# An RWKV-5 attention and MLP kernel in one program: weights loaded as whole rows, one interleaved pair instead of two, more turns by DMA, a new hand-written order

## The chip, the cores and the metric

One core of one Trainium2 chip runs the whole program. The metric is device time in microseconds (us), the median of several runs. The profile shown is of one execution; its times count from that execution's first instruction.

## The reference

For each of 4 batches and 8 heads (head width 48, 768 positions) a state of 48 x 48 decays by `w` and takes up `k` times `v` at every position; `r` reads it. The result, 384 wide, then goes through a layer norm and a two-layer MLP with a residual.

```python
for t in range(S):
    cur = einsum('bhd,bhe->bhde', u[None] * k[t], v[t])
    y[t] = einsum('bhd,bhde->bhe', r[t], state + cur)
    state = w[None, :, :, None] * state + einsum('bhd,bhe->bhde', k[t], v[t])
x = y as (4, 768, 384)
xn = (x - mean(x)) / sqrt(var(x) + 1e-6) * g_ln
out = x + maximum(xn @ w_ch1, 0) @ w_ch2          # 384 -> 1536 -> 384
```

## The kernel before

The 3072 positions are cut into 24 chunks (tiles) of 128, six to a batch. All inputs are fp32 in memory, the matmuls run in bf16. The program is a list of steps, `PLAN`, written out by hand; each entry is `name,index,engine`, with `s` for ACT, `v` for DVE, `g` for POOL, `-` for PE or a DMA issued by SP. Every engine takes its steps in the order of that list. So the list sets all that is queued behind what.

**Loading.** `LK`, `LR` and `LV` (L352, L355, L358) fetch one chunk of k, r or v, 192 KB in runs of 192 bytes. `LK2`, `LR2`, `LV2` (L371, L374, L377) fetch two chunks at once, 384 KB, and put two neighbouring positions on one partition, so that a run is 384 bytes. Pairs below `PAIRS` are kept in that interleaved order through the whole attention (`AT2`, `Y2`, `AM2`, L435, L497, L523); from there on only r comes in pairs, and `TCr` (L411) puts it back in order while it copies the turned r out of PSUM.

**Attention of a chunk.** `SK`/`SR` (and `SKH`, `SRH`, `SR2` for interleaved pairs) scale k and r. Both are then turned: by PE (`TRk`, `TRr`, L400) with a copy out of PSUM (`TCk`, `TCr`), or by a DMA (`TDk` L422, `TDr` L427). `AT` is the score matmul, `AM` its mask, `S` the state update and the bonus sums (copied by `CC2`), `ZU`/`ZD` the decayed state, `Y` the output, `X` adds the bonus term.

**MLP of a tile.** `XN` centres x and `SQ` sums its squares. x is turned by PE and copied (`LT` L627, `XT` L633) or by a DMA (`LTD` L621). `UP` (L637) is one PSUM bank of the first matmul: 12 matmuls for a group of one tile, 6 wider ones for a group of two. Step number is 16 x group + bank. `RL` (L654) takes the bank out through a relu, on ACT or DVE. There are two such banks. `DN` (L666) is four matmuls of the second layer, and step number is 4 x tile + third. `RS` (L610) makes the reciprocal deviation: on ACT as an `Ln` and an `Exp` (L613, L614), on POOL as a power. `OT` applies it and adds x, `STO` stores.

**Weights.** `LW1` (L334) fetches a third of the first weight, 768 KB; `SW` (L337) scales a ninth of it to bf16: step i is for columns n = i / 3 and input rows kc = i mod 3. `UP` with bank n of a one-tile group needs the three `SW` of that n. `IW2` (L348) fetches a third of the second weight from POOL's queue with a cast.

**Start.** `WF` fetches w, `LN` takes its logarithm on ACT (L284), `WBM` spreads it by a matmul, and `FK2`, `FR2`, `FK`, `FR`, `WL` take `Exp` of multiples of it. `DU` steps are matmuls on zeros that keep PE busy. `TL` (L231) is one instruction on ACT, in the ninth place of the list, ahead of `LN`:

```python
    def TL(i, e):
        nc.scalar.preload_act_table_set("natural_log_exp_and_others")
```

Of the kernel before, what the change touches and what calls it, by code (L numbers as in the profile page):

```python
# [21 lines left out]
TCk,0,s TRr,1,- LV2,1,- CV2,0,s UW,0,v Q2,0,v AT2,0,- DU,1536,- FR,0,s TCr,1,v LK,4,- WL,0,s SR2,2,g AM2,0,v S,0,- AT2,1,-
LK,6,- CC2,0,s DU,512,- ZU,0,v TRk,1,- AM2,1,v DU,512,- VB2,0,g S,1,- TCk,1,s LK,7,- DU,512,- TRr,2,- LW1,1,- SR2,3,v DU,512,-
Y2,1,- TCr,2,s LW1,2,- LV,5,- Q2,1,v Y2,0,- SK,4,g ZU,1,v UGC,0,s LV,4,- CV2,1,s X,1,v TRr,3,- SK,5,g X,0,v DU,512,-
AT2,3,- TCr,3,s DU,512,- AM2,3,v SK,7,g S,2,- XN,1,s AT2,2,- XN,0,g CC2,1,v ZU,2,v SQ,1,s DU,512,- VB2,1,g TRk,2,- AM2,2,v
S,3,- LW1,0,- TCk,2,s DU,512,- SK,6,v LT,1,- Y2,2,- SQ,0,s SW,5,g XT,1,v SW,3,s LV,6,- LT,0,- SW,4,v TRk,3,- Q2,2,g
ZU,3,v DU,1024,- SW,6,s LK,8,- XT,0,v Y2,3,- SW,7,s TCk,3,v X,2,v SW,8,s AT,5,- AT,4,- X,3,v XN,2,g DU,512,- UP,2,-
AM,5,v XN,3,s IW2,0,g LV,7,- UP,1,- RL,2,s Q2,3,g AM,4,v LT,2,- CV2,2,s DU,512,- UP,17,- RL,1,s XT,2,v S,4,- RL,17,s
LR2,4,- UP,34,- SW,0,v SW,2,s AT,6,- CC2,2,v ZU,4,v SW,1,s VB2,2,g AT,7,- AM,6,v LK,9,- Y,4,- RL,34,s UP,0,- IW2,1,g
X,4,v UP,18,- RL,0,s AM,7,v IW2,2,g Y,5,- XN,4,s LT,3,- UP,32,- RL,18,s RS,1,g LV,8,- X,5,v LT,4,- UP,33,- RL,32,s  # L30
XT,3,v XN,5,g DU,512,- CV2,3,v LV,9,- UP,16,- RL,33,s XT,4,v SK,8,v S,6,- DN,0,- SR2,4,v CC2,3,s RL,16,s UP,48,- SQ,5,s
ZU,6,v UP,64,- VB2,3,v RL,48,s TRr,4,- SQ,3,s Y,6,- SK,9,g DN,1,- RS,3,s X,6,v RL,64,s UP,66,- RS,0,g TDk,4,- SQ,2,s
DN,2,- RS,2,g LT,5,- S,7,- OT,0,v RL,66,s UP,49,- XN,6,s XT,5,v UP,50,- RL,49,v TCr,4,s LR2,6,- DN,4,- ZU,7,v UP,80,-
ZD,7,v LK,10,- CV2,4,g RL,50,v Y,7,- RL,80,s DN,5,- X,7,v LV,13,- DN,6,- Q2,4,v XN,7,s UP,65,- SQ,4,s OT,1,v LV,11,-
AT,8,- SQ,6,s SR2,6,v AT,9,- DN,8,- RS,6,s LR2,5,- AM,8,v RS,4,s DN,9,- SQ,7,s LK,11,- S,8,- DN,10,- ZU,8,v LV,10,-
UP,82,- CC2,4,s OT,2,v VB2,4,g LK,12,- LT,6,- AM,9,v Y,8,- RL,82,s DN,12,- STO,0,- RL,65,s SK,10,g DN,13,- XT,6,v LK,13,-
X,8,v DN,14,- ZD,8,g LV,12,- S,9,- UP,96,- OT,3,v SK,11,g ZU,9,v UP,98,- RL,96,s SR2,5,v Y,9,- TDk,5,- SQ,8,s DN,16,-
CV2,5,v LT,7,- TRr,5,- SK,12,v DN,17,- X,9,v TCr,5,s RL,98,v LK,15,- UP,97,- XN,9,g LK,14,- XT,7,v ZD,9,g UP,81,- RL,97,s
LR2,7,- XN,8,s SK,13,g UP,112,- RL,81,s LTD,8,- DN,18,- RS,7,s Q2,5,v TRr,6,- OT,4,v UP,114,- SK,15,g TCr,6,s RL,112,v STO,1,-
S,10,- CV2,6,g DN,20,- CC2,5,s TDk,6,- RL,114,s SK,14,v AT,10,- RS,5,s AT,11,- ZU,10,v DN,21,- SR2,7,g AM,10,v UP,113,- STO,3,-  # L40
DN,22,- AM,11,v RL,113,s TDk,7,- Y,10,- VB2,5,g UP,129,- OT,5,v TRr,7,- RL,129,s LR,19,- UP,130,- ZD,10,g X,10,v UP,133,- LV,14,-
Q2,6,v RL,130,s DN,24,- TCr,7,v STO,2,- S,12,- DN,25,- CC2,6,s LV,15,- XN,10,s VB2,6,g ZU,12,v AT,12,- SQ,9,s AT,13,- STO,5,-
AM,12,v Y,11,- RL,133,s DN,26,- Q2,7,g LK,16,- X,11,v UP,128,- OT,6,v XN,11,s Y,12,- UP,131,- X,12,v LK,17,- DN,28,- AM,13,v
SR,19,g CV2,7,s S,13,- DN,29,- LTD,9,- ZU,13,v SQ,12,s DN,30,- ZD,13,g RL,128,s Y,13,- OT,7,v AT,15,- SQ,11,s LR2,8,- AT,14,-
X,13,v UP,132,- STO,4,- SK,17,g RL,131,v SQ,13,s LR,18,- S,14,- AM,15,v LV,17,- XN,13,s DN,32,- LV,16,- XN,12,s DN,33,- ZU,14,v
RL,132,s SK,16,v UP,144,- CC2,7,v AM,14,v LTD,10,- VB2,7,g UP,147,- RL,144,s DN,34,- SQ,10,s SR2,8,v TDk,8,- Y,14,- RS,8,s UP,145,-
RL,147,s OT,8,v TRr,8,- ZD,14,v UP,148,- TCr,8,s RL,145,v RL,148,v DN,36,- LK,18,- X,14,v DN,37,- CV2,8,v XN,14,s S,15,- UP,149,-
ZU,15,v LK,19,- UP,161,- ZD,15,g RL,149,v LV,18,- DN,38,- RL,161,s Q2,8,v STO,7,- Y,15,- LV,20,- UP,146,- SK,18,g X,15,v STO,6,-
AT,16,- RL,146,s AT,17,- XN,15,v LR,20,- UP,164,- RS,9,g OT,9,v LTD,11,- AM,17,v UP,160,- RL,164,s RS,10,g DN,40,- RL,160,v S,16,-
SK,19,v UP,163,- SR,18,v CC2,8,s TDk,9,- UP,165,- ZU,16,v RL,163,s AM,16,v DN,41,- ZD,16,g RL,165,s DN,42,- VB2,8,g LR,21,- UP,162,-  # L50
OT,10,v TDr,9,- Y,16,- RL,162,v DN,44,- X,16,v DN,45,- XN,16,g UP,176,- LV,19,- SR,20,g DN,46,- RL,176,s STO,8,- Y,17,- OT,11,v
UP,178,- LK,20,- X,17,v DN,48,- Q2,9,v LK,21,- UP,177,- XN,17,g SR,21,v DN,49,- LTD,12,- RL,177,s RL,178,v DN,50,- CV2,9,v AT,19,-
OT,12,v AT,18,- SK,20,g STO,9,- UP,180,- AM,18,v STO,11,- S,18,- SK,21,g RL,180,s UP,181,- CC2,9,v ZU,18,v DN,52,- VB2,9,g AM,19,v
RL,181,s STO,10,- UP,179,- SQ,16,s TDk,10,- DN,53,- RL,179,s Y,18,- SQ,17,s TDr,10,- DN,54,- X,18,v UP,194,- OT,13,v UP,195,- STO,12,-
RL,194,s LK,23,- Y,19,- SQ,14,s DN,56,- LR,23,- X,19,v SQ,15,s DN,57,- XN,18,s RS,11,g UP,197,- RL,195,s DN,58,- XN,19,s S,19,-
RL,197,s LTD,13,- UP,196,- OT,14,v SQ,19,s Q2,10,v DN,60,- RL,196,s ZU,19,v LV,21,- UP,193,- LR,22,- ZD,19,g LK,22,- UP,192,- RL,193,s
SK,23,g AT,20,- SQ,18,s STO,13,- AT,21,- AM,20,v LV,22,- DN,61,- RL,192,s SR,23,g LV,23,- RS,12,s DN,62,- CV2,10,g UP,208,- OT,15,v
UP,210,- AM,21,v RL,208,s DN,64,- SR,22,v S,20,- RL,210,v UP,212,- TDr,11,- CC2,10,v DN,65,- SK,22,v VB2,10,g ZU,20,v DN,66,- Y,20,-
TDk,11,- OT,16,v UP,209,- X,20,v DN,68,- RL,209,s ZD,20,v STO,14,- S,21,- XN,20,g RL,212,v CV2,11,s DN,69,- LTD,14,- ZU,21,v SQ,20,s
DN,70,- UP,213,- RS,13,s OT,17,v STO,16,- UP,211,- STO,15,- Y,21,- RL,211,s DN,72,- X,21,v DN,73,- Q2,11,v SQ,21,s AT,23,- ZD,21,v  # L60
RL,213,s AT,22,- XN,21,v S,22,- LTD,15,- UP,224,- ZU,22,v AM,22,v DN,74,- ZD,22,g RL,224,s UP,226,- CC2,11,s RS,14,s OT,18,v VB2,11,g
UP,225,- AM,23,v STO,18,- DN,76,- RL,225,s Y,22,- RL,226,s DN,77,- X,22,v DN,78,- XN,22,g UP,240,- LTD,16,- OT,19,v Y,23,- RL,240,s
DN,80,- X,23,v STO,17,- UP,242,- XN,23,v STO,19,- SQ,23,s LTD,17,- DN,81,- RL,242,s DN,82,- SQ,22,s UP,257,- RS,17,s OT,20,v RS,16,g
UP,241,- RL,257,s RS,15,g DN,84,- RL,241,s UP,258,- DN,85,- RL,258,v UP,256,- DN,86,- RL,256,v UP,272,- OT,21,v UP,273,- STO,21,- DN,88,-
RL,273,v DN,89,- RL,272,v DN,90,- UP,274,- OT,22,v DB,0,- STO,22,- RL,274,s DB,1,- STO,20,- DA,0,- DB,2,- DA,1,- OB,23,v DA,2,-
# [5 lines left out]
def kernel(  # L71
# [122 lines left out]

    psum = {}
# [135 lines left out]
                func=ACT.Exp, scale=float(L),  # L331
            )

    def LW1(n, e):  # L334
        nc.sync.dma_start(out=w1_f[n][:], in_=w1_src[:, n])

    def SW(i, e):  # L337
        n, kc = divmod(i, CK)
        o, s = w1_sb[n][kc][:], w1_f[n][:, kc]
        g = g_neg[:, kc : kc + 1]  # L340
        if e == "s":
            nc.scalar.activation(out=o, in_=s, func=ACT.Copy, scale=g)  # L342
# [440 lines left out]
```

## Time and profile before

| | us |
|---|---|
| median of 3 runs | 149.03 (148.55 to 149.23) |
| span of the profiled execution | 147.5 |
| PE busy | 141.5 |
| DVE busy | 112.3 |
| ACT busy | 82.4 |
| POOL busy | 72.0 |

Busy time of an engine is the time in which one of its instructions ran; PE's contains the matmuls on zeros, and its matmuls overlap, so that the mean duration of one is longer than the step from one to the next. The chain of waits goes back from the last instruction to what released each piece of work; its pieces of PE work give the time that a step takes when PE runs without a pause. "SPq" is SP issuing DMAs.

### The profile page before, as it was taken

To read this page: it belongs to the slowest core of one execution; us is meant where nothing else is said; L and a number is where in the kernel's file an instruction comes from. 1 tells how busy PE (TensorE), PEld (TensorE's weight loads), DVE (VectorE), ACT (ScalarE), POOL (GpSimd) and SP (SyncE) were. 2 spreads that over 40 slices of the span, in tenths; PEclk is the share of its full clock that TensorE was granted. 3 is DMA by queue.
4 is the path that set the end of the run, shared out by engine and by line. 5 is a ranking of instruction groups with operands and counts; after the bars stand their busy time and mean duration, and the time that the engine had idled before them with its cause. 6 is when DMAs were issued, how large, how long until landed. Compare 5 with 4: busy or idle time off the path is not lost.

```text
span 147.5 us, 4689 instructions
## 1 busy us (share of the span) xinstructions
PE 141.5 (96%) x1943; PEld 111.1 (75%) x1943; DVE 112.3 (76%) x206; ACT 82.4 (56%) x181; POOL 72.0 (49%) x96
## 2 busy tenths in 40 slices
...
GB/s 112 300 242 240 192 339 187 283 243 215 220 95 231 202 225 165 264 205 258 164 192 196 195 235 124 173 204 227 197 112 191 182 142 154 82 46 119 8 99 111
DMA packets 85097, 27.18 MB, mean 184 GB/s; under 512 B 80338, under 2 KB 83540, under 8 KB 85076
## 3 DMA queue, kind: packets, MB, share of 16 engines
...
q0 software_dynamic: 432, 1.18, 4.3%
q8 instruction: 15, 0.25, 0.7%
q14 instruction: 6, 0.05, 0.1%
q10 hardware_dynamic: 2, 0.00, 0.0%
HBM read 18.88 MB, written 4.72 MB: 160 GB/s over the span
## 4 chain that ended last, share of the span: by engine, by line
PE 65%; SPq 13%; DMA 11%; DVE 6%; POOL 1%; issue 1%; DVEq 0%
PE o L674 28%; PE hp L646 25%; DMA kf<-in_k_dram 6%; DMA w_f<-in_moe_w_ch_dram 5%; SPq L374 4%; SPq L352 3%; PE at L544 3%; PE y L583 2%; SPq L358 2%; PE y L481 2%; PE y L575 2%; SPq L371 1%; SPq L377 1%; DVE hT L664 1%; PE y L460 1%
## 5 line engine op out<-in xcount | busy, mean ns | idle before, releaser
L646 PE MATMUL hp<-xT,w_sb 128*128 128x128 bf16 (+1 forms) x648 | 57.1, 237 | 0.8 <-ACT w_sb L342 0.7
L662 ACT ACTIVATE hT<-hp 128x512 bf16<-128x512 f32 x55 | 32.4, 594 | 40.5 <-PE hp L646 39.7
L646 PEld LDWEIGHTS <-w_sb 128*128 128x128 bf16 x648 | 49.3, 114 | 5.1 <-ACT w_sb L342 1.3
L674 PE MATMUL o<-w_sb,hT 128*128 128x384 bf16 x276 | 53.0, 326 | 0.0
L674 PEld LDWEIGHTS <-hT 128*128 128x128 bf16 x276 | 25.0, 97 | 12.0
L553 DVE TENSOR_TENSOR A<-at,mask 128x1024 bf16<-128x1024 f32 x20 | 24.2, 1216 | 2.1 <-PE at L544 2.1
L492 POOL TENSOR_TENSOR Vb<-vf,cc 128x768 f32<-128x768 f32 x11 | 16.5, 1498 | 14.9 <-ACT cc L200 8.5
L730 DVE SCALAR_TENSOR_TENSOR ot<-o,rs,x 128x384 f32<-128x384 f32 x23 | 14.1, 615 | 12.3 <-PE o L674 7.0
L205 POOL TENSOR_TENSOR sk<-kf,Fk 128x384 bf16<-128x384 f32 x13 | 13.6, 1053 | 8.5 <-DMA kf<-in_k_dram 7.9
L597 ACT ACTIVATE sqj<-x,sm 128x384 bf16<-128x384 f32 x24 | 14.6, 609 | 2.2 <-DVE x L590 2.2
L205 POOL TENSOR_TENSOR Z<-ZS,WLZ 128x384 bf16<-128x384 f32 x8 | 8.0, 1002 | 15.4 <-DVE ZS L565 15.4
L590 DVE SCALAR_TENSOR_TENSOR x<-y,Vb 128x384 f32<-128x384 f32 x20 | 11.0, 552 | 4.5 <-PE y L583 4.1
L664 DVE TENSOR_SCALAR hT<-hp 128x512 bf16<-128x512 f32 x17 | 11.5, 684 | 3.4 <-PE hp L646 3.3
L279 PE MATMUL o<-warm 128*128 128x512 bf16 x33 | 11.3, 427 | 1.0 <-DVE warm L228 1.0
L200 ACT COPY trr<-at 128x512 bf16<-128x512 bf16 (+1 forms) x13 | 9.1, 764 | 4.4 <-PE at L400 4.4
L205 DVE TENSOR_TENSOR sr<-rf,Fr 128x768 bf16<-128x768 f32 (+1 forms) x11 | 9.5, 870 | 1.6 <-DMA rf<-in_r_dram 1.6
L205 POOL TENSOR_TENSOR sr<-rf,Fr 128x384 bf16<-128x384 f32 (+1 forms) x5 | 6.6, 1325 | 7.0 <-DMA rf<-in_r_dram 7.0
L604 ACT ACTIVATE xn<-x,sm 128x384 bf16<-128x384 f32 x13 | 7.8, 609 | 2.3 <-DVE x L590 2.3
L606 POOL TENSOR_SCALAR xn<-x,sm 128x384 bf16<-128x384 f32 x8 | 5.3, 665 | 7.6 <-DVE x L590 7.5
L205 DVE TENSOR_TENSOR q<-trk,trr 128x1024 bf16<-128x1024 bf16 x9 | 7.5, 837 | 1.4 <-ACT xn L604 1.0
L481 PE MATMUL y<-vv,sk 128*128 128x96 bf16 (+1 forms) x96 | 7.3, 204 | 0.3 <-ACT vv L200 0.2
L205 DVE TENSOR_TENSOR sk<-kf,Fk 128x384 bf16<-128x384 f32 (+1 forms) x10 | 7.4, 747 | 0.0
...
## 6 DMA issues: line engine op xcount, KB each, us to landing
...
```

The lines of the kernel that those rows point to most:

```text
L205: engines[e].tensor_tensor(out=out, in0=in0, in1=in1, op=ALU.mult)
L279: nc.tensor.matmul(out=warm_ps[0][:].rearrange("p (a t) -> p a t", a=4), lhsT=warm[:], rhs=rhs, start=True, stop=True)
L481: nc.tensor.matmul(out=t[:, q * E2 : (q + 1) * E2].rearrange("p (e d) -> p e d", e=2), lhsT=lhs, rhs=rhs, start=first, stop=True, skip_gro ...
L492: engines[e].tensor_tensor(out=Vb2(g).rearrange("p (x h d) -> p x h d", x=2, h=H), in0=vals, in1=cc2(g)[:].unsqueeze(3).to_broadcast([P, 2 ...
L553: nc.vector.tensor_tensor(out=AA(i)[:].rearrange("p e q t -> p (e q) t"), in0=psum["at", i][:].rearrange("p e q t -> p (e q) t"), in1=mask ...
L590: nc.vector.scalar_tensor_tensor(out=xx(i)[:], in0=psum["y", i][:, :C], scalar=1.0, in1=Vb(i), op0=ALU.mult, op1=ALU.add, accum_out=sm[i][:],)
L597: nc.scalar.activation(out=sqj[:], in_=xx(i)[:], func=ACT.Square, bias=sm[i][:], scale=-float(C), accum_out=sq[g][:, j : j + 1])
L646: nc.tensor.matmul(out=t[:, a * gw : (a + 1) * gw], lhsT=w1_sb[n][kc][:, fb::FB], rhs=xT(g)[:, :size, kc, :], start=(kc == 0), stop=(kc == ...
L662: nc.scalar.activation(out=o, in_=s, func=ACT.Relu)
L664: nc.vector.tensor_relu(out=o, in_=s)
L674: nc.tensor.matmul(out=psum["o", i][:, :C], lhsT=hT(g)[:, fk, j * P : (j + 1) * P], rhs=w2_sb[d][:, a, :], start=(fk == 0), stop=(fk == FK ...
L730: nc.vector.scalar_tensor_tensor(out=ot(i)[:], in0=psum["o", i][:, :C], scalar=rs[g][:, j : j + 1], in1=xx(i)[:], op0=ALU.mult, op1=ALU.add,)
```

## The change

- `PAIRS` is 1 instead of 2: only chunks 0 and 1 are kept interleaved. Chunks 2 and 3 come as single loads of k and v, with `AT`, `Y`, `AM`; their r still comes as a pair and is put in order by `TCr`.
- The first weight is fetched as whole rows: `LW1,kc` takes 128 rows of 1536 numbers (768 KB) instead of a third of the columns of all rows. The bytes are the same, but any `SW` of a column third now needs the row block that it is in, so the first `UP` needs all three loads.
- The list is new. The three `LW1` stand behind the first pair's loads, k of chunks 2 and 3 and (two of them) v of chunks 2 and 3. `IW2,1` and `IW2,2` stand near the start of POOL's steps.
- r of chunks 12 to 17 comes as single loads and is turned by `TDr` 6, 7, 8; `TRr` and `TCr` 6, 7, 8 go. Tiles 6 and 7 are turned by `LTD`; `LT` and `XT` 6, 7 go.
- `XT` 0 to 4 move from DVE to ACT; `SW` runs 7 times on ACT and twice on POOL (before: 6 on ACT, 2 on DVE, 1 on POOL).
- `TL` stands in the middle of the list, behind `RL,149`, instead of ahead of `LN`. Between `LN` and `TL` the list has `RS` on ACT for groups 1, 0, 3, 4, 2, 5 and 9.

```diff
-PAIRS = 2
+PAIRS = 1
...
+ML,0,v WF,0,s LN,0,s MI2,0,g MW,0,v MO,0,v DU,3072,- WBM,0,- FK2,0,s MM,0,g MP,0,g MP,1,g FR2,0,s MZ,0,v MP,2,g MM2,0,g MP,4,g
+LK2,0,- MP,3,g FK2,1,s LR2,0,- UF,0,- LV2,0,- LR2,1,- LK,3,- LG,0,- LK,2,- LW1,1,- LV,2,- LV,3,- LW1,0,- LW1,2,- LR2,2,- LK,4,-
+LK,5,- LV,4,- LK,7,- LV,5,- UWR,0,v DU,4096,- COL,0,- FR2,1,s SKH,1,v MI,0,g FR,0,s FK,0,s SRH,0,v CV2,0,v SRH,1,v UW,0,s
+UGC,0,s WL,0,s SKH,0,g IW2,1,g SR2,1,g IW2,2,g MP,5,g SK,2,g SK,3,g TRk,0,- TCk,0,v DU,512,- TRr,0,- TCr,0,v DU,1536,- AT2,0,-
+Q2,0,v DU,512,- S,0,- AT2,1,- CC2,0,s AM2,0,v ZU,0,v VB2,0,g IW2,0,g CV2,1,g S,1,- TRr,1,- AM2,1,v Y2,0,- ZU,1,v X,0,v TRk,1,-
+SW,7,s SW,4,s TCr,1,s TCk,1,v Q2,1,v SW,0,g SW,1,g Y2,1,- SR2,2,g AT,3,- X,1,v XN,0,s LT,0,- XT,0,s S,2,- AT,2,- SQ,1,s XN,1,s
+CC2,1,s ZU,2,v DU,1536,- S,3,- AM,2,v SW,3,s RS,1,s SQ,0,s ZU,3,v LT,1,- Y,2,- XT,1,s SW,2,s SW,5,s UP,1,- VB2,1,v AM,3,v X,2,v
+RL,1,s UP,16,- UP,0,- RL,16,s DN,4,- TRr,2,- Y,3,- XN,2,g SK,4,g RL,0,v X,3,v SK,5,v XN,3,g CV2,2,g SW,6,s SW,8,s LT,2,- UP,17,-
...
+AM,5,v UP,32,- SK,7,v RL,32,v SK,6,g Y,4,- LT,3,- SQ,2,s XT,3,s TRr,3,- UP,2,- VB2,2,g X,4,v RL,2,s TRk,3,- Y,5,- UP,49,- DN,2,-
+TCr,3,v XN,4,s SQ,3,s TCk,3,s LT,4,- UP,48,- XT,4,s RS,0,s X,5,v RL,49,v Q2,3,v OT,0,v CV2,3,g SK,9,g SR2,4,g SK,8,g UP,33,-
+AT,6,- AT,7,- RL,48,s S,6,- RL,33,s CC2,3,s RS,3,s SQ,4,s RS,4,s DN,8,- DN,9,- XN,5,g VB2,3,g AM,6,v ZU,6,v AM,7,v Y,6,- TRr,4,-
+UP,64,- DN,10,- X,6,v RL,64,s TCr,4,s TDk,4,- LT,5,- Y,7,- UP,50,- LV,9,- LV,8,- LK,11,- XT,5,v UP,80,- XN,6,v X,7,v XN,7,v
+RL,50,s RS,2,s OT,2,v AT,8,- AT,9,- S,7,- ZU,7,v Q2,4,v AM,9,v SK,10,g SK,12,g RL,80,s SR2,5,g ZD,7,g CV2,4,s SK,11,v AM,8,v
+UP,66,- UP,65,- DN,12,- RL,66,s S,8,- SQ,6,s RL,65,s UP,81,- RL,81,s CC2,4,s LV,12,- LTD,6,- STO,0,- LK,13,- LTD,7,- TDk,5,-
...
+ZU,10,v SR,13,g RL,112,s UP,113,- LTD,8,- STO,1,- UP,128,- CC2,5,s SQ,8,s RS,5,s RL,113,s SQ,7,s RL,128,s DN,26,- TDk,6,-
+TDr,6,- LK,15,- LR,14,- LV,13,- LK,14,- SR,15,v VB2,5,g ZD,10,g UP,131,- Y,10,- UP,114,- RL,114,s RL,131,s OT,6,v X,10,v DN,20,-
...
+Y,13,- OT,7,v X,13,v XN,13,g TDk,7,- TDr,7,- UP,145,- UP,146,- S,13,- LK,17,- LK,16,- STO,6,- LTD,10,- STO,7,- LR,17,- RL,145,s
+SQ,12,s SQ,13,s RL,146,s RS,9,s DN,40,- UP,147,- AT,14,- AT,15,- UP,149,- Q2,7,g ZU,13,v CV2,7,v S,14,- RL,147,s RL,149,s TL,0,s
...
-    w1_f = [const.tile([P, CK, FW], FP32, name=f"w1_f{n}") for n in range(NW)]
+    w1_f = [const.tile([P, F], FP32, name=f"w1_f{kc}") for kc in range(CK)]
...
-    w1_src = moe_w_ch1.rearrange("(kc p) (n f) -> p n kc f", p=P, n=NW)
+    w1_src = moe_w_ch1.rearrange("(kc p) f -> p kc f", p=P)
...
-    def LW1(n, e):
-        nc.sync.dma_start(out=w1_f[n][:], in_=w1_src[:, n])
+    def LW1(kc, e):
+        nc.sync.dma_start(out=w1_f[kc][:], in_=w1_src[:, kc])
...
-        o, s = w1_sb[n][kc][:], w1_f[n][:, kc]
+        o, s = w1_sb[n][kc][:], w1_f[kc][:, n * FW : (n + 1) * FW]
```

78 lines of the change are left out of this document (30 added, 48 removed).

## The prediction

> **What bounds the kernel now.** I read the chain of waits first, then the chain in order of time, then the windows.
>
> ```profile
> span 147.5 us, 4689 instructions
> PE 65%; SPq 13%; DMA 11%; DVE 6%; POOL 1%; issue 1%; DVEq 0%
> ```
>
> PE is two thirds of the chain. The rest of the chain (SP's issues and DMA) is the start.
>
> ```profile
> 26.10 0.25 PE L646 MATMUL hp<-xT,w_sb 128*128 128x128 bf16 x1
> 28.97 0.83 PE L646 MATMUL hp<-xT,w_sb 128*128 128x128 bf16 x12
> 46.87 0.55 PE at L544 x16
> 48.83 0.18 PE y L460 x8
> 49.01 0.19 PE y L481 x4
> 49.20 0.65 PE o L674 x4
> 49.85 0.67 PE hp L646 x12
> 50.52 0.17 PE at L631 x3
> 50.69 0.17 PE y L575 x4
> 50.86 0.20 PE y L583 x8
> 59.64 0.45 PE at L400 x8
> 70.55 0.65 PE hp L646 x6
> 143.08 0.33 PE o L689 x4
> 144.44 0.42 DVE ot L705
> ```
>
> The first two rows (timeline) are the first `UP` matmul, at 26.10, and the end of the third `UP`, `UP,17`, at 29.80. The others (chain) are what each step costs when PE runs without a pause: `UP` 0.67 (one tile) or 0.65 (two), `DN` 0.65, two `AT` 0.55, `S` 0.18 for its bonus sums and 0.19 for its state, `LT` 0.17, `Y` 0.17 + 0.20, a `TR` 0.45, a half `DN` 0.33. I counted what the old list has behind `UP,17`: 33 x 0.67 + 36 x 0.65 `UP`, 69 `DN`, 18 `AT`, 20 `Y`, 16 `S`, 5 `TR`, 5 `LT`, 6 halves: 112.4 us. PE took from 29.8 to 144.4, so 114.6. From about 30 us on PE has gaps of only 2.2 us in all, and 3.1 us follow its last step. **The bound is PE's remaining work, counted from when `UP` starts in earnest.**
>
> **The new list on the same scale.** Behind its first `UP` (`UP,1`) stand 36 x 0.67 + 36 x 0.65 `UP`, 69 `DN`, 20 `AT`, 21 `Y`, 16 `S`, 6 `TR`, 4 `LT`, 6 halves: 115.6 us. The three `TRr` (1.35) and two `LT` (0.34) that go are already left out of it. With the same gaps and the same end the span is T + 115.6 + 2.2 + 3.1 = **T + 120.9**, where T is the time of `UP,1`; it ties with 147.5 at T = 26.6.
>
> **When the weights are there.** `UP,1` needs `SW` 3, 4 and 5, so all three row blocks.
>
> ```profile
> 0.00:5.00 5.00, 4.03 (x11) 1.73 (x12) 1.75 (x9) 2.00 (x3) 4.09 (x22) 1.00 0.62 161
> 5.00:10.00 5.00, 4.55 (x66) 2.87 (x64) 3.81 (x8) 4.22 (x7) 0.64 (x5) 1.00 1.03 257
> 10.00:15.00 5.00, 4.71 (x81) 3.02 (x79) 4.43 (x7) 3.03 (x6) 2.85 (x2) 1.00 1.01 252
> 15.00:20.00 5.00, 5.00 (x138) 3.69 (x136) 4.71 (x10) 4.22 (x8) 2.98 (x4) 1.00 0.97 220
> 20.00:25.00 5.00, 4.74 (x115) 3.46 (x113) 4.82 (x8) 2.63 (x6) 3.96 (x5) 1.00 0.98 296
> 25.00:30.00 5.00, 4.23 (x78) 3.36 (x73) 4.35 (x9) 4.34 (x8) 4.96 (x4) 1.00 0.92 240
> 30.00:35.00 5.00, 5.00 (x107) 4.80 (x106) 4.55 (x11) 4.10 (x8) 3.51 (x6) 1.00 1.13 235
> 35.00:40.00 5.00, 5.00 (x85) 4.41 (x83) 3.96 (x8) 3.98 (x12) 0.78 (x1) 1.00 1.13 217
> L335 SPq DMA_DIRECT2D w_f<-in_moe_w_ch_dram x3: 486/769/5583, 15.9 to 19.6; - x3
> DMA to landing us min/median/max: 7.4/8.6/9.8
> ```
>
> The last column of the windows is GB/s. From 5 to 30 us the mean is 253, and 0.8 MB have moved before. The old list has 6.29 MB ahead of and in its last `LW1`: 5 + 5.49 / 253 = 26.7; it landed at 19.6 + 9.8 = 29.4, 2.7 late. The new list has, up to `LW1,2`, four pair loads (1.57 MB), four single loads (0.79), the weight (2.36) and, on POOL's queue beside it, the second weight (1.18): 5.90 MB, so 5 + 5.09 / 253 = 25.1. But the second weight is read as fp32 and counted as bf16: in the two windows in which it moved, 30 to 40 us, the rate was 235 and 217, which is 1.1 us lost: **26.2**. Bounds: 28.9 with the lateness of the old one; 20.5 if the second weight's bytes all come behind. I take 26.2, since fewer loads queue behind it. The row block before it lands some 2 us sooner, as the first two loads did (15.9 + 7.4 and, by the median of 8.6, about 25.3): 24.2. That the first weight moves in runs of 6 KB instead of 2 KB I count as nothing to 1.5 us of gain: the 20-25 us window, the one with most weight bytes, has 296 GB/s against 253.
>
> ACT then has, in list order, `SW,3`, `RS,1`, `SQ,0`, `XT,1`, `SW,2`, `SW,5`, and `UP,1` waits behind the last.
>
> ```profile
> L662 ACT ACTIVATE hT<-hp 128x512 bf16<-128x512 f32 x55 | 32.4, 594 | 40.5 <-PE hp L646 39.7
> L597 ACT ACTIVATE sqj<-x,sm 128x384 bf16<-128x384 f32 x24 | 14.6, 609 | 2.2 <-DVE x L590 2.2
> L597 ACT ACTIVATION_READ_ACCUMULATOR sqj<-x,sm 128x1 f32 x24 | 4.6, 190 | 0.0
> L604 ACT ACTIVATE xn<-x,sm 128x384 bf16<-128x384 f32 x13 | 7.8, 609 | 2.3 <-DVE x L590 2.3
> L342 ACT ACTIVATE w_sb<-w_f,g_neg 128x512 bf16<-128x512 f32 x6 | 4.0, 713 | 2.2 <-DMA w_f<-in_moe_w_ch_dram 2.2
> L613 ACT ACTIVATE rs<-sq,epsc 128x1 f32<-128x1 f32 x7 | 2.1, 295 | 0.1
> L614 ACT ACTIVATE rs<-rs 128x1 f32<-128x1 f32 x7 | 1.4, 203 | 0.2
> 17.89 1.34 ACT L200 COPY trr<-at 128x512 bf16<-128x512 bf16 x2 [0.47 <-PE at L400]
> L200 ACT COPY cc<-y 128x16 f32<-128x16 f32 x7 | 1.2, 173 | 3.4 <-PE y L481 2.9 <-DVE ZS L565 0.5
> ```
>
> `SW` is 0.71, `SQ` 0.80 (609 + 190 ns), `RS` 0.50 (295 + 203), `RL` 0.59, a `TCr` two copies with 1.34 from start to end, `CC2` 0.17. `XT` on ACT is in no row; between 0.59 and 0.71 (the rows around it) I take 0.6, the row of that size (L604). So 24.2 + 0.71 + 0.50 + 0.80 + 0.6 = 26.8, then two `SW`: T = 28.2, and T + 120.9 = **149.1, with nothing else changed**: the earlier weights are used up by the wait for all three and by PE having done less before them.
>
> **The table load.** This is where I see the change decided.
>
> ```profile
> 1.26 1.28 ACT L231 ACT_TABLE_LOAD   x1 [1.26 <-PEq L767]
> 2.55 0.52 ACT L284 ACTIVATE ln_all<-w_row 1x384 f32<-1x384 f32 x1
> ```
>
> The old run has one table load, x1, 1.28 us, ahead of ACT's first `Ln`; the `RS` on ACT (seven in the two rows above, three more for groups of two) then run `Ln` and `Exp` with nothing between (idle before the seven 0.1 and 0.2 us in all). The new list has this instruction behind `RL,149`. `LN`, the `Exp` steps and seven `RS` stand before it. No row shows what stands in front of an `Ln` when the named set is not loaded. Lower bound: one load serves all, nothing added. Upper bound: a load made for an `Ln` brings no `Exp` and the other way round; then each change from one to the other is a load: `LN`, `FK2`, 7 x 2, and `TL`, 17 loads. I take the upper bound, because the program asks for its set by a name with both functions in it, while a load made on need knows only the function that needs it. Per load I take 1.28; with the idle time in its own row, 1.26, the most is 2.54.
>
> The first two cost nothing: `LN` has its load where `TL` was, and the `Exp` load lies beside `WBM`. Each of the seven `RS` grows from 0.50 to 0.50 + 2 x 1.28 = 3.07, and what queues behind it on ACT are `RL`s; PE has two banks, so it stops at the third `UP` or at a `DN` that needs the relu. Place by place, PE's work until it must wait against ACT's until it lets it go:
>
> - `RS,1`: ahead of `UP,1`, PE has nothing else: **2.6**. T = 30.8.
> - `RS,0`: PE from the end of `UP,48`: `UP,33`, two `AT`, `S,6`, `DN,8` = 2.2, then `DN,9` needs `RL,33`. ACT: `XT,4`, `RS`, two `RL` = 4.9, begun 0.7 sooner: 4.2. Loss **2.0**.
> - `RS,3`, `RS,4`: PE has `DN,9`, `Y,6`, `TRr,4`, `UP,64`, `DN,10`, `LT,5`, `Y,7`, `UP,50` = 3.8, then no bank. ACT: `CC2`, `RS`, `SQ`, `RS`, `RL,64` = 7.7. Loss **3.9**.
> - `RS,2`: `UP,66` starts at 2.1, then `UP,65` needs `RL,80`, at 1.34 + 0.59 + 3.07 + 0.59 = 5.6; without the loads 3.0. Loss **2.6**.
> - `RS,5`: `UP,131` needs `RL,113`; PE has 0.65 of other work, ACT is late by 1.4 without the loads already. Loss **2.6**.
> - `RS,9`: PE has 3.1 until `DN,41` needs `RL,147`, ACT 5.8, without the loads 3.2. Loss **2.6**.
> - `TL` itself: two `DN`, `S,15`, two `UP` hide 1.28. Nothing.
>
> Sum 16.3. From below: behind `UP,1` up to `TL` the list has 53.6 us of PE and 44.6 of ACT (with `TL`); six `RS` make ACT 60.0, so if every wait were shared the loss is 2.6 + 6.4 = 9.0. From above, with 2.54 a load, 33. I take 16.3, since the row of L662 shows 39.7 us of waits for PE: ACT follows PE bank by bank, with no stock to live on.
>
> The Trainium skill, page "ScalarE: Activation LUTs", section "What ACT_TABLE_LOAD costs", gives 1283 ns for the load, as the row here, and about 1380 ns of drain with it for a switch. The row shows `LN` 0.01 us behind the load, so no drain behind it; one ahead of it no run here shows. By 2.66 us a switch the estimate would be 14 x 1.38, some 19 us more.
>
> **The rest, costed at nothing.**
>
> ```profile
> trr<-sr SPq DMA_TRANSPOSE x3, 4.9
> xT<-xn SPq DMA_TRANSPOSE x10, 3.0
> ```
>
> `TDr` 6 to 8 and `LTD` 6, 7 take 4.9 and 3.0 us to land, and stand 5 to 6 us of PE's work ahead of their use; `LTD,6` waits for `XN,6` with a store, `LK,13`, `LTD,7`, `TDk,5` and r of pair 6 behind it on SP. Five pair loads become ten single loads, twice the runs for the same bytes, while SP also has five more turns. A slower PE gives these more room; without that cover up to 2 us at each of the five turns. Three `TCr` less free ACT of 4.0 us where it waits for PE anyway.
>
> **The sum.** 30.8 + 120.9 + (2.0 + 3.9 + 2.6 + 2.6 + 2.6 = 13.7) = 165.4 us of span. The median of the runs is 149.03 for 147.5 of span, 1.5 more: **166.9**.
>
> **The rivals.**
>
> - **One load serves all.** Against it: the named set. For it: nothing in the trace speaks of loads on need. T = 28.2, span 149.1, **150.6 us**; 145 to 154 by the bounds of the landing. The Trainium skill, page "ScalarE activation tables: per-element evaluation and per-set limits", section "Table sets in the compiler and the runtime", says that loads are placed block by block, by the greedy longest run; by that rule this is the case. No row of the old run can show it. Chance 0.07.
> - **Faster: one load serves, and the weights come early.** The place is ACT's `SW,2` and `SW,5`. At the 296 GB/s of the 20-25 window the last block lands at 22.2, T = 24.2, span 145.1, **146.6 us**. It decides where T is below 26.6. Against it: the second weight shares the engines. Chance 0.04.
> - **A load costs twice**, by the 2.54 above: 14 more loads x 1.26 = 17.6 on ACT and, as ACT has no stock, on PE: **184 us**. Against it: the idle time in that row ends with PE's sequencer, not with the load. Chance 0.07.
>
> **How the numbers follow.** Forecast 0.82, rivals 0.07, 0.04, 0.07. The forecast's own range is 153 to 178 (T between 25 and 33.5, losses behind it between 6.4 and 22). To leave out no more than 2 in 10 the range goes up to 180. A measurement of this kernel tells 0.5% from no change. Faster: 0.05 (rival two and a part of rival one); the same: 0.02, of rival one; slower: 0.93.
>
> **What would show it.** 17 `ACT_TABLE_LOAD` instead of 1, and ACT's busy time up by some 16 us net; `UP,1` near 30.8; six waits of PE of 2 to 4 us on ACT's `RL` before `TL`, and none like them behind it, where PE runs as densely as before. I am wrong if the loads are one or two, if PE's gaps before `TL` are below 6 us in all, or if SP's queue, not ACT, ends PE's waits.

## The result and the profile after

| | us | against the old kernel, same chip |
|---|---|---|
| before, median of 4 runs | 149.13 (148.55 to 150.71) | |
| after, median of 4 runs | 174.06 (172.35 to 176.35) | 1.165, 95% interval 1.156 to 1.174 |
| span of the profiled execution | 172.9 (before 147.5) | |

Some executions take a few per cent longer than the others of the same kernel; a ratio is of the others, measured beside the old kernel on the same chip, and a median is of all. The time is inside the forecast's range (153 to 180) and 7.2 us above its 166.9. One item of the change was miscounted ahead of the prediction, and the prediction reads it so too: the new list has `SW,5,v`, so that step runs on DVE (six `SW` on ACT, one on DVE, two on POOL), and not behind `SW,2` on ACT.

The page of the new kernel, its first lines, the clock and the chain of waits by engine. Lines of code from L200 on are one lower than before.

```profile
span 172.9 us, 4475 instructions
PE 149.1 (86%) x1822; PEld 114.3 (66%) x1822; DVE 110.9 (64%) x191; ACT 98.3 (57%) x195; POOL 85.8 (50%) x110
PEclk9996558699996996999999999999999999999999
PE 35%; ACT 24%; DVE 13%; DMA 13%; SPq 6%; issue 6%; POOL 1%; ACTq 0%; DVEq 0%; POOLq 0%
```

PE's share of the chain falls from 65% to 35% and ACT, which was not in it, has 24%. ACT is busy for 98.3 us instead of 82.4. The clock row is new: PE's granted clock, which was full in all of the old run, falls to about half after 13 us and again three times.

The groups of ACT with shapes kept apart (count, busy us, mean ns, idle time before):

```profile
L612 ACT ACT_TABLE_LOAD x7 | 9.0, 1283 | 0.1
L613 ACT ACT_TABLE_LOAD x7 | 9.0, 1283 | 0.1
L283 ACT ACT_TABLE_LOAD x1 | 1.3, 1283 | 2.1 <-DMA w_row<-in_w_dram 2.1
L300 ACT ACT_TABLE_LOAD x1 | 1.3, 1283 | 1.8 <-PE hp L287 1.8
L230 ACT ACT_TABLE_LOAD x1 | 1.3, 1283 | 0.0
```

Seventeen loads instead of one: two at each of the seven `RS` ahead of `TL`, one for `LN`, one for the first `Exp`, and `TL`'s own. The timeline of ACT shows one such place, and PE's shows who waits for it:

```profile
47.73 1.28 ACT L612 ACT_TABLE_LOAD   x1
49.03 0.29 ACT L612 ACTIVATE rs<-sq,epsc 128x1 f32<-128x1 f32 x1
49.34 1.28 ACT L613 ACT_TABLE_LOAD   x1
50.64 0.20 ACT L613 ACTIVATE rs<-rs 128x1 f32<-128x1 f32 x1
50.74 1.06 ACT L661 ACTIVATE hT<-hp 128x512 bf16<-128x512 f32 x2
```

```profile
28.04 0.84 PE L645 MATMUL hp<-xT,w_sb 128*128 128x128 bf16 x12
30.03 0.27 PE L645 MATMUL hp<-xT,w_sb 128*128 128x128 bf16 x2 [1.15 <-ACT xT L199]
51.55 1.76 PE L673 MATMUL o<-w_sb,hT 128*128 128x384 bf16 x5 [1.97 <-DVE ot L729]
64.55 0.99 PE L645 MATMUL hp<-xT,w_sb 128*128 128x128 bf16 x12 [2.72 <-ACT hT L661]
82.25 0.85 PE L645 MATMUL hp<-xT,w_sb 128*128 128x256 bf16 x6 [1.68 <-DMA xT<-xn]
86.19 0.82 PE L645 MATMUL hp<-xT,w_sb 128*128 128x256 bf16 x6 [2.45 <-ACT hT L661]
```

`RS,0` takes 3.1 us on ACT from 47.73 to 50.84, and the two relus stand behind it. PE is stopped there by `OT,0` on DVE, which needs `RS,0` and holds the one output bank. The first `UP` is at 28.04; the next, `UP,16`, waits for `XT,1`, which stands behind `RS,1` with its two loads. At 61.8 to 64.6 and 83.7 to 86.2 PE waits for a relu, behind the loads of `RS,2` and of `RS,5`. One wait, at 82.25, is ended by a DMA turn.

The windows in which the clock fell (PE, PEld, DVE, ACT and POOL busy; then the granted clock):

```profile
30.00:35.00 5.00, 4.62 (x47) 3.79 (x47) 1.17 (x4) 3.04 (x6) 1.56 (x2) 0.66 1.07 232
50.00:55.00 5.00, 3.46 (x24) 2.07 (x24) 3.65 (x5) 4.93 (x10) 3.04 (x3) 0.66 0.97 190
65.00:70.00 5.00, 5.00 (x50) 3.92 (x48) 4.02 (x6) 3.14 (x9) 1.92 (x2) 0.66 0.29 52
```

0.66 in a window of 5 us is half clock for (1 - 0.66) x 5 / 0.5 = 3.4 us. The first follows the wait at 30.03, the second that at 51.55, the third that at 64.55. At the start it is longer: the four windows from 10 to 30 us have 0.89, 0.50, 0.50 and 0.75, so 13.6 us. Number 1 below has 0.84, 0.50, 0.98 and 1.00 there, 6.8 us.

The start itself is later too. The first `Exp` and `SW,5`, on which the first `UP` waits, in the new kernel:

```profile
6.95 0.58 ACT L300 ACTIVATE Fk<-hp,pow 128x384 f32<-128x384 f32 x1
27.53 0.48 DVE L343 TENSOR_SCALAR w_sb<-w_f,g_neg 128x512 bf16<-128x512 f32 x1
```

And in number 1 below, which has no load between `LN` and this `Exp`:

```profile
5.50 0.58 ACT L300 ACTIVATE Fk<-hp,pow 128x384 f32<-128x384 f32 x1 [2.43 <-PE hp L287]
25.59 0.48 DVE L343 TENSOR_SCALAR w_sb<-w_f,g_neg 128x512 bf16<-128x512 f32 x1
```

PE's waits over the whole run (us in total, times, longest):

```profile
PE hp L645 <- ACT hT L661: 6.8, 4, 2.7
PE o L673 <- ACT hT L661: 1.4, 1, 1.4
```

To place the losses I use one measure. The **lag** of a relu is its start, less T (the first `UP`), less what PE's steps in the list cost from the first `UP` up to this relu's own, at the prices of the prediction. A step of the lag is time that PE lost there. For the old kernel it ends at 3.7, for the new one at 25.8; T is 26.1 and 28.0, and the work 114.6 and 115.6. So +25.4 of span is 1.9 + 22.1 + 1.0, and 0.4 at the end.

### The profile page after: what moved, and what is told of

It is laid out like the page before. It is cut to its first block, busy times and chain, and to the rows that moved or that the text cites. A ratio compares the mean times of both kernels' runs of the same rounds, so it can differ in the third digit from the quotient of the medians.

```text
span 172.9 us, 4475 instructions
## 1 busy us (share of the span) xinstructions
PE 149.1 (86%) x1822; PEld 114.3 (66%) x1822; DVE 110.9 (64%) x191; ACT 98.3 (57%) x195; POOL 85.8 (50%) x110
## 4 chain that ended last, share of the span: by engine, by line
PE 35%; ACT 24%; DVE 13%; DMA 13%; SPq 6%; issue 6%; POOL 1%; ACTq 0%; DVEq 0%; POOLq 0%
PE hp L645 12%; PE o L673 10%; DMA kf<-in_k_dram 6%; ACT L612 5%; ACT L613 4%; ACT sqj L596 4%; ACT hT L661 3%; DMA rf<-in_r_dram 2%; DMA xT<-xn 2%; DVE q L204 2%; PE at L399 2%; DVE A L552 2%; DVE sk L204 2%; SPq L622 2%; DMA trk<-sk 2%
## 5 line engine op out<-in xcount | busy, mean ns | idle before, releaser
L645 PE MATMUL hp<-xT,w_sb 128*128 128x128 bf16 (+1 forms) x648 | 59.0, 242 | 10.0 <-ACT hT L661 6.8
L661 ACT ACTIVATE hT<-hp 128x512 bf16<-128x512 f32 x60 | 35.0, 593 | 39.2 <-PE hp L645 38.8
L673 PEld LDWEIGHTS <-hT 128*128 128x128 bf16 x276 | 26.1, 100 | 18.9 <-issue 5.2
L552 DVE TENSOR_TENSOR A<-at,mask 128x1024 bf16<-128x1024 f32 x22 | 26.5, 1214 | 0.0
L204 POOL TENSOR_TENSOR sr<-rf,Fr 128x384 bf16<-128x384 f32 (+1 forms) x15 | 19.7, 1314 | 9.8 <-DMA rf<-in_r_dram 9.8
L491 POOL TENSOR_TENSOR Vb<-vf,cc 128x768 f32<-128x768 f32 x8 | 12.1, 1516 | 15.7 <-ACT cc L199 14.2
L605 POOL TENSOR_SCALAR xn<-x,sm 128x384 bf16<-128x384 f32 x11 | 7.0, 634 | 18.9 <-DVE x L589 18.8
L204 POOL TENSOR_TENSOR Z<-ZS,WLZ 128x384 bf16<-128x384 f32 x8 | 9.2, 1147 | 10.8 <-DVE ZS L564 10.8
L663 DVE TENSOR_SCALAR hT<-hp 128x512 bf16<-128x512 f32 x12 | 8.2, 687 | 6.4 <-PE hp L645 6.4
L204 DVE TENSOR_TENSOR sk<-kf,Fk 128x384 bf16<-128x384 f32 x10 | 8.2, 824 | 5.5 <-DMA kf<-in_k_dram 2.8
L278 PE MATMUL o<-warm 128*128 128x512 bf16 x22 | 8.6, 530 | 1.4 <-DVE warm L227 1.4
L199 ACT COPY cc<-y 128x16 f32<-128x16 f32 x9 | 1.5, 170 | 14.5 <-PE y L480 7.9
L613 ACT ACT_TABLE_LOAD x7 | 9.0, 1283 | 0.1
L612 ACT ACT_TABLE_LOAD x7 | 9.0, 1283 | 0.1
L201 POOL CAST vv<-vf 128x768 bf16<-128x768 f32 x6 | 5.3, 875 | 6.6 <-PE hp L645 3.8
```

The source lines that it names most:

```text
L204: engines[e].tensor_tensor(out=out, in0=in0, in1=in1, op=ALU.mult)
L278: nc.tensor.matmul(out=warm_ps[0][:].rearrange("p (a t) -> p a t", a=4), lhsT=warm[:], rhs=rhs, start=True, stop=True)
L491: engines[e].tensor_tensor(out=Vb2(g).rearrange("p (x h d) -> p x h d", x=2, h=H), in0=vals, in1=cc2(g)[:].unsqueeze(3).to_broadcast([P, 2 ...
L552: nc.vector.tensor_tensor(out=AA(i)[:].rearrange("p e q t -> p (e q) t"), in0=psum["at", i][:].rearrange("p e q t -> p (e q) t"), in1=mask ...
L612: nc.scalar.activation(out=rs[g][:], in_=sq[g][:], func=ACT.Ln, scale=1.0 / C, bias=epsc[:])
L613: nc.scalar.activation(out=rs[g][:], in_=rs[g][:], func=ACT.Exp, scale=-0.5)
```

## The experiments

Theory: the table loads carry most of the loss. Rivals: the earlier weights and the cold start; the DMA turns and SP's queue; the new order by itself. Of a line of the list the diffs show only the part that changes. A time "in one run" is of a single execution, and a span is always of one.

**1. The load first.** The new kernel with `TL` back ahead of `LN`.

```diff
-ML,0,v WF,0,s LN,0,s
+ML,0,v WF,0,s TL,0,s LN,0,s
...
-RL,149,s TL,0,s
+RL,149,s
```

> The new kernel with the named table load ahead of LN again. Theory (the 16 extra loads, with the clock falls that PE's waits bring, are the loss): one load in the run, span near T + 120.9 with T near 28, so 149 us of span and 150.6 us; no fall of the granted clock behind 35 us. Rival (the rest of the change, above all the DMA turns and the loads by chunk, costs as much as the loads): one load, but still above 158 us, with PE waiting for DMAs behind 70 us.

156.97 us (154.69 to 158.71, 4 runs), ratio 1.040 (1.026 to 1.055); span 154.4, 5 above the theory's 149. Of ACT's groups and of the page:

```profile
L230 ACT ACT_TABLE_LOAD x1 | 1.3, 1283 | 1.3 <-PEq L766 1.3
PE 40%; DVE 18%; SPq 15%; DMA 14%; issue 6%; POOL 3%; ACT 2%; POOLq 0%; DVEq 0%; ACTq 0%
```

One load is left, ACT's share of the chain falls to 2%, and 18.5 us of span go. The late load is the cause of 18.5 of the 25.4 us. The rest, 6.9, isn't.

**2. The loads taken away in another manner.** `TL` stays late, and the seven `RS` ahead of it run as powers on POOL.

```diff
-RS,1,s
+RS,1,g
...
-RS,9,s
+RS,9,g
```

> The new kernel with the load where it stands, but RS of groups 1, 0, 3, 4, 2, 5 and 9 on POOL as a power: 3 loads instead of 17, LN's and the first Exp's among them. Theory: it is the Ln/Exp changes that cost, not the place of the load, so the time is within 3 us of e1_load_first (some more POOL work, 7 x 0.8 us). Rival (something else about the late load, or ACT's order, costs): above 158 us.

160.0 us in one run, span 158.2, 3 loads (`LN`, the first `Exp`, `TL`). The gain comes without touching `TL`, so it is the change between `Ln` and `Exp` that is paid, not the place of the instruction. It is 3.0 us (3.8 of span) above number 1, at the edge of what the theory allowed. Of these 3.8, 1.8 are T, with no load of an `RS` ahead of it:

```profile
27.90 2.36 PE L645 MATMUL hp<-xT,w_sb 128*128 128x128 bf16 x36
```

The other 2.0 are lag behind T; whether the powers on POOL make it no run here shows.

**3. The same fault in the old kernel.** `TL` behind the old list's seventh `RS` on ACT, nothing else.

```diff
-UF,0,- TL,0,s MO,0,v
+UF,0,- MO,0,v
...
-RS,12,s DN,62,-
+RS,12,s TL,0,s DN,62,-
```

> The old kernel with nothing changed but the named load moved behind its seventh RS on ACT. Theory: 17 loads, each of the seven RS 2.57 us longer, and ACT has no stock there either: 149 + 7 x 2 to 3 = 163 to 170 us, with falls of the clock where PE waits long. Rival (the old order has enough slack on ACT, its waits for PE are 40 us): below 156 us.

163.68 us in one run, span 161.9: 14.4 us more for 16 more loads. T stays at 26.1 and the lag ends at 18.2 instead of 3.7. PE's timeline and the windows:

```profile
55.99 0.48 PE L575 MATMUL y<-Z,trr 128*128 128x96 bf16 x4 [3.74 <-ACT cc L200]
```

```profile
55.00:60.00 5.00, 4.01 (x23) 2.25 (x23) 0.57 (x2) 1.91 (x7) 3.98 (x4) 0.51 0.14 28
60.00:65.00 5.00, 5.00 (x62) 4.22 (x61) 4.23 (x9) 1.63 (x4) 1.21 (x3) 0.80 0.65 126
```

A wait of 3.74 us, and half clock for 4.9 + 2.0 = 6.9 us, in a kernel that had none.

**4. One place alone.** The old list with `TL` directly behind its first `RS` on ACT (`RS,3`): three loads in a row, ahead of `RL,64`.

```diff
-UF,0,- TL,0,s MO,0,v
+UF,0,- MO,0,v
...
-RS,3,s X,6,v
+RS,3,s TL,0,s X,6,v
```

> The old list with TL directly behind its first RS on ACT (RS,3): 5 table loads, two of them for LN and the first Exp, and three (3.85 us) in a row ahead of RL,64; the other six RS run without loads. Theory, each load ahead of a relu is paid at its place: the 14.5 us of lag that seven pairs brought are 2.1 a pair, here with TL's own 1.28 up to 3.4, so the span is 149.5 to 151 and the time 1.014 to 1.023 of the old. Rival, most of those 14.5 us came from the granted clock that fell behind the waits, and a single wait brings no fall: span below 149, 1.00 to 1.01.

152.44 us (6 runs), ratio 1.023 (1.016 to 1.030); span 150.3. ACT's and PE's timelines and the window behind the wait:

```profile
39.01 1.28 ACT L613 ACT_TABLE_LOAD   x1
40.61 1.28 ACT L614 ACT_TABLE_LOAD   x1
42.13 1.28 ACT L231 ACT_TABLE_LOAD   x1
```

```profile
44.07 0.83 PE L646 MATMUL hp<-xT,w_sb 128*128 128x128 bf16 x12 [2.69 <-ACT hT L662]
45.15 0.83 PE L646 MATMUL hp<-xT,w_sb 128*128 128x128 bf16 x12 [0.25 <-ACT hT L662]
```

```profile
45.00:50.00 5.00, 4.85 (x76) 4.01 (x75) 4.44 (x9) 4.09 (x9) 1.31 (x2) 1.00 1.13 256
```

Three loads give waits of 2.69 and 0.25 us. From `UP,48` to `UP,80` the lag rises by 3.2 (0.2 in the old kernel): 3.0 us, 1.0 a load, and nothing of it comes back. The clock stays at 1.00, so the loads cost by themselves; the rival that the clock makes most of the loss falls.

PE's waits above 0.15 us, added up from the first `UP` on, say the same for the rest. In number 3 they are 11.5 us instead of the old kernel's 0.7, so 10.8 of its 14.5 us of lag; the other 3.7 are near what a half clock for 6.9 us can cost at most (6.9 / 2 = 3.4). The new kernel has 15.6 and number 1 has 4.5: 11.1 by waits, at most 3 x 3.4 / 2 = 5.1 by the clock behind T, and 1.9 in T: 18.1 of 18.5.

**5. A warm and earlier start.** Number 1 with more matmuls on zeros in the start.

```diff
-DU,512,- TRr,0,- TCr,0,v DU,1536,- AT2,0,-
+DU,6144,- TRr,0,- TCr,0,v DU,1536,- AT2,0,-
...
-Q2,0,v DU,512,- S,0,-
+Q2,0,v DU,2048,- S,0,-
```

> e1_load_first with 5632 and 1536 more columns of matmuls on zeros in the two places of the start where PE waited 2.4 and 0.9 us. Theory on the clock (a wait of PE of some us is what lets the granted clock fall to a half): no fall between 14 and 28 us, Y2, TR and S of the start at full speed, T 1 to 3 us sooner and the time 1 to 3 us below e1_load_first. Rival (the weights' landing at 23 us sets T, or the fall has another cause): no change within 1 us.

160.19 us (158.66 to 165.96, 4 runs), ratio 1.072 (1.054 to 1.090); span 156.9, 2.5 above number 1. T is 24.2, 1.9 sooner, as expected; the time isn't shorter, as the theory had it, but longer. PE's timeline and the window behind it:

```profile
25.58 3.16 PE L645 MATMUL hp<-xT,w_sb 128*128 128x128 bf16 x34 [1.10 <-DVE w_sb L343]
```

```profile
25.00:30.00 5.00, 4.42 (x42) 3.77 (x43) 3.65 (x6) 3.14 (x5) 3.38 (x3) 0.66 0.97 193
```

The half clock of the start is gone. But the first `UP` stops after two of its 12 matmuls: its third weight, `SW,5`, has to wait for the last landing, at 25.0. So the weights hold the start here, as the rival said. The clock falls behind that wait instead, and the lag is 4.9 by `UP,32` (1.9 in number 1). The early T was worth nothing in this list.

**6. Rows alone.** The old kernel with the first weight as whole rows (the lines of `w1_f`, `w1_src`, `LW1` and `SW` in the change), the list as it was.

```diff
-    def LW1(n, e):
-        nc.sync.dma_start(out=w1_f[n][:], in_=w1_src[:, n])
+    def LW1(kc, e):
+        nc.sync.dma_start(out=w1_f[kc][:], in_=w1_src[:, kc])
...
-        o, s = w1_sb[n][kc][:], w1_f[n][:, kc]
+        o, s = w1_sb[n][kc][:], w1_f[kc][:, n * FW : (n + 1) * FW]
```

> The old kernel with the first weight as whole rows, the loads left where they stood. Theory: all three must land before the first UP; the last landed at 29.4, then four SW on ACT (2.8 us), so T goes from 26.1 to about 32, the span from 147.5 to 152 to 154, and with a fall of the granted clock behind the wait to 156. Rival, rows of 6 KB land sooner than pieces of 2 KB: last landing at 27 or before, T about 30, span 150 to 152.

154.38 us in one run, span 152.6; the last block landed at 27.9 (29.4 before). PE's timeline and the windows:

```profile
29.35 0.29 PE L646 MATMUL hp<-xT,w_sb 128*128 128x128 bf16 x1 [3.95 <-ACT w_sb L342]
```

```profile
25.00:30.00 5.00, 0.73 (x7) 0.24 (x3) 2.85 (x6) 2.04 (x4) 4.97 (x4) 0.82 1.01 253
30.00:35.00 5.00, 4.68 (x40) 4.22 (x41) 0.75 (x2) 2.91 (x5) 0.29 (x1) 0.50 1.08 231
```

The span is as the theory said, T (29.35) nearer to the rival's 30 than to 32: the landing was 1.4 us sooner, part of it because the issue was 0.3 to 0.8 us sooner too. T costs 3.3 of the 5.1 us; the other 1.9 is lag behind it, with half clock for 6.8 us.

**7. More DMA turns alone.** The old kernel with r of chunks 12 to 15 as single loads turned by `TDr`, and tiles 6 and 7 turned by `LTD`; the diff shows r of pair 6 and tile 6, the others alike.

```diff
-LR2,6,-
+LR,12,- LR,13,-
...
-SR2,6,v
+SR,12,v SR,13,v
...
-TRr,6,- OT,4,v UP,114,- SK,15,g TCr,6,s RL,112,v
+TDr,6,- OT,4,v UP,114,- SK,15,g RL,112,v
...
-XN,6,s
+XN,6,s LTD,6,-
...
-LT,6,- AM,9,v
+AM,9,v
```

> The old kernel with r of chunks 12 to 15 as single loads turned by DMA and tiles 6 and 7 turned by DMA, nothing else changed. Theory, the turns hide and PE's work is the bound: PE loses 2 x 0.45 + 2 x 0.17 = 1.24 us of work, so the span is 146.3 and the time 1.2 us below the old one (0.992). Rival, the turns are exposed or hold SP's queue: up to 2 us at each of the four, so up to 7 us above the old one (1.00 to 1.045).

155.05 us (154.10 to 157.47, 6 runs), ratio 1.042 (1.036 to 1.047); span 153.3: 5.8 more, although PE has 1.24 us less to do. The clock is 1.0 throughout. SP's part of the timeline, old kernel first, then this one, and what DVE waited for from 40 to 82 us:

```profile
51.36 0.65 SPq L740 DMA_DIRECT2D out_dram<-ot  x1
```

```profile
54.45 0.62 SPq L740 DMA_DIRECT2D out_dram<-ot  x1
```

```profile
DVE ot L730 <- DMA out_dram<-ot: 3.5, 2, 2.4
DVE q L205 <- DMA trk<-sk: 3.3, 1, 3.3
```

The first store is issued 3.1 us later, and `LTD,8`, the old kernel's first turn of a tile, 5.4 later (64.07 for 58.67). DVE then waits for stores that free `ot` and for `trk`, and PE waits for DVE.

**8 and 9. Its two halves.** Only the tiles (the last two hunks of that diff, for 6 and 7), and only r (the first three).

> The first half of the kernel with four more DMA turns: the old one with only tiles 6 and 7 turned by DMA (LTD 6, 7; LT and XT 6, 7 go). Theory, SP's queue is a resource that was full: each turn takes 1.2 to 1.5 us of SP's time and moves all that is behind it, so about half of the 7.5 us of lag that the four turns brought is here and the span is 149 to 151.5. Rival, it is the r turns and their single loads: this one hides and saves 0.34 us, span 147 to 148.5.

> The other half: the old kernel with only r of chunks 12 to 15 as single loads turned by DMA (TDr 6, 7). Theory, SP's queue is full: two more loads (0.6 us each) and two more turns (1.25 us each) on SP, about half of the 7.5 us of lag, less 0.9 us of PE's work: span 148.5 to 151. Rival, the tile turns did it all: span 146.5 to 147.5.

Tiles: 152.70 us (4 runs), ratio 1.025 (1.019 to 1.031), span 150.5. r: 152.58 us (4 runs), ratio 1.016 (1.007 to 1.026), span 150.6. Each costs 3.0 to 3.1 us of span and together 5.8, so it is not one of them alone. Both put the first store later, the tiles by 2.7 us and r by 1.4 (52.71), which fits the time on SP that each takes. Of the first:

```profile
45.86 3.02 SPq L623 DMA_TRANSPOSE xT<-xn  x1
54.03 0.65 SPq L740 DMA_DIRECT2D out_dram<-ot  x1
```

One turn holds SP for 3.02 us, and the store of 51.36 is at 54.03.

**10 and 11. The turns taken back in the new list.** Number 1 with `LT` and `XT` 6, 7 for `LTD`; and with `TRr` and `TCr` 6 to 8 for `TDr`, `TCr` as a plain copy.

```diff
-LTD,6,-
...
-DN,13,- DN,14,- ZU,8,v
+DN,13,- LT,6,- DN,14,- XT,6,v ZU,8,v
```

```diff
-TDr,6,-
+TRr,6,- TCr,6,s
```

> The kernel with the table load first, with tiles 6 and 7 turned by PE again (LT, XT 6, 7 on PE and DVE, LTD 6, 7 taken out). Theory, SP's queue carries a part of the 5.5 us of lag that the new order still has: SP gets 2.5 us at 50 to 55 us, the gaps at 55 to 70 us shrink by 1 to 2.5 us, span 152 to 153.7. Rival, the new order's own sequence on DVE and ACT holds that stretch: PE and DVE get 0.34 and 0.70 us more, span 154.4 to 156.

> The kernel with the table load first, with r of chunks 12 to 17 turned by PE and copied by ACT again (TRr, TCr 6 to 8 in the places of TDr). Theory, the DMA turns were hidden: PE gets 3 x 0.45 = 1.35 us more work and ACT 4.0 us more, so the span goes from 154.4 to 155.5 to 158. Rival, the turns by DMA are a part of the 5.5 us that this kernel still loses against the old one: span 150 to 153.5.

Tiles by PE: 158.17 us (4 runs), ratio 1.060 (1.056 to 1.064), span 155.9; the rival held. r by PE: 162.41 us in one run, span 160.6, above what either expected. In the second ACT stands idle ahead of the new copies:

```profile
90.74 1.01 ACT L199 COPY trr<-at 128x1024 bf16<-128x1024 bf16 x1 [5.38 <-PE at L399]
```

It waits for PE's turn with relus behind it, so this run prices the copies where I put them and not the turns. What the first shows is that PE's turns of the tiles give nothing back in the new list; for r the question stays open.

**12. One place of the new order.** In number 1 PE has a gap of 1.80 us up to 68.37, which ends with `RL,113`. `CC2,5` stands behind `ZU,10`, and ACT waits 2.5 us for it. I put `CC2,5` ahead of `ZU,10`, and the two relus ahead of `SQ,8` and `RS,5`.

```diff
-ZU,10,v SR,13,g RL,112,s UP,113,- LTD,8,- STO,1,- UP,128,- CC2,5,s SQ,8,s RS,5,s RL,113,s SQ,7,s RL,128,s DN,26,-
+RL,112,s CC2,5,s ZU,10,v SR,13,g UP,113,- LTD,8,- STO,1,- UP,128,- RL,113,s RL,128,s SQ,8,s RS,5,s SQ,7,s DN,26,-
```

> The kernel with the table load first (156.97 us, span 154.4), with ACT's order mended at one place: CC2,5 ahead of ZU,10 and RL,113, RL,128 ahead of SQ,8 and RS,5. Order theory: the 2.13 us gap of PE at 66.25, which ends with RL,113, comes from CC2,5 (ACT waits 2.54 us for DVE's ZS) and from SQ,8 and RS,5 (1.3 us) ahead of the relu; it goes, the lag at UP,131 falls from 6.3 to about 4, and the span is 152.0 to 152.7, 154 to 155.5 us. Rival, the loss is only moved to the next wait (DMA turns or OT): span 154 or more, 156.5 us or more.

156.17 us (153.79 to 156.53, 4 runs), ratio 1.042 (1.029 to 1.055); span 154.7. The runs lie across both expectations and overlap those of number 1. PE's timeline:

```profile
64.24 1.46 PE L673 MATMUL o<-w_sb,hT 128*128 128x384 bf16 x8 [1.22 <-DVE ot L729]
68.13 0.85 PE L645 MATMUL hp<-xT,w_sb 128*128 128x256 bf16 x6 [1.40 <-DMA xT<-xn]
```

The wait for the relu is gone, and `OT` and a DMA turn take its place with 1.22 and 1.40 us. The lag at `UP,131`, which was to fall from 6.3 to about 4, is 6.9: in this profile the loss moved, as the rival said.

## Why the prediction came out as it did

The time is in the range, but the parts of its sum are off, and one against the other: without the loads T came 2.1 us sooner than forecast, the gaps and the end took 7.4 more, and the loads 2.2 more.

**Seventeen loads of 1.28 us: right.** The count, the places and the duration are those of the prediction, and ACT's busy time is up by 15.9 us for "some 16". The Trainium skill, page "ScalarE: Activation LUTs", section "What ACT_TABLE_LOAD costs", gives the same 1283 ns but some 1380 ns of drain with it. The trace doesn't agree with the drain: in the rows above `Ln` starts 0.02 us behind its load, and the next load 0.02 us behind the `Ln`. The rival by which one load serves all fell: no run here with `TL` late showed fewer than a load at each change. The Trainium skill, page "ScalarE activation tables: per-element evaluation and per-set limits", section "Table sets in the compiler and the runtime", says that loads are placed by the greedy longest run, which the prediction read as this rival. The trace, with 17, doesn't agree with that reading.

**What they cost, 16.3: 18.5.** The difference between the new kernel and number 1, place by place (steps of T plus lag):

| place | forecast | measured |
|---|---|---|
| first `Exp` (T) | 0 | 1.9 |
| `RS,1` (up to `UP,32`) | 2.6 | 3.6 |
| `RS,0` (up to `UP,48`) | 2.0 | 2.7 |
| `RS,3`, `RS,4` (up to `UP,50`) | 3.9 | 3.2 |
| `RS,2` (up to `UP,97`) | 2.6 | 2.9 |
| `RS,5` (up to `UP,131`) | 2.6 | 3.5 |
| `RS,9`, `TL` (up to `UP,165`) | 2.6 | 1.4 |
| behind | 0 | -0.7 |

Behind T the steps hold within 1.2 us, but two paths were others than the prediction's. `RS,1` was to hold up `UP,1`; `SW,5` is on DVE, so `UP,1` doesn't wait for `RS,1`. `UP,16` does, and the clock fell behind it (0.66 in the 30 to 35 window). At `RS,0` it named `DN,9` and `RL,33`, and PE was stopped at `DN,8` by `OT,0` and the one output bank. The size came out near because both wait for the same `RS`, which is luck. The prediction has no term for the clock either, which is at most 5.1 us of these steps.

The 1.9 us of T are the first `Exp`'s load, which the prediction put at nothing because it "lies beside `WBM`". Its row says that it stands behind `WBM`'s result (1.8 `<-PE hp L287`), and the first `Exp` starts 1.45 us later than in number 1. In number 2, which has this load and none ahead of an `RS`, T is 27.9. Numbers 1, 11, 12 and 10, with the same start and `TL` first, have 26.1, 25.6, 26.6 and 26.8. The half clock of the start lasts 6.8 us in 1 and 11, and 13.6 or 13.7 in 12, 10, 2 and the new kernel. So against a start with as long a half clock the load costs 1.1 to 1.5 us, near its 1.28; the rest goes with the clock.

**T without loads, 28.2: 26.1.** The weights landed at 13.3, 20.8 and 23.0 in the new kernel, and the last at 25.1 in number 1, where I had 24.2 and 26.2 for the last two (bounds 20.5 to 28.9). The rate was mis-sized, as the windows of the new kernel show (last column, GB/s):

```profile
5.00:10.00 5.00, 4.99 (x54) 2.43 (x52) 2.04 (x4) 4.32 (x9) 2.65 (x4) 1.00 1.19 259
10.00:15.00 5.00, 2.31 (x34) 1.31 (x35) 4.96 (x6) 0.93 (x4) 3.98 (x5) 0.89 1.08 275
15.00:20.00 5.00, 4.74 (x77) 3.60 (x76) 2.92 (x4) 2.60 (x5) 2.82 (x3) 0.50 1.05 335
```

The mean is 290 where I took 253. But the landing isn't what set T. `SW,5` starts at 27.53 in the new kernel, 4.5 us behind it, and at 25.59 in number 1, each time directly behind `ZU,3` on DVE: the attention of the first chunks set T, and the ACT steps that I put behind the landing (`RS,1`, `SQ,0`, `XT,1`, `SW,2`) aren't on the way to `UP,1`. Of the runs of the new list only number 5, with that attention made faster, shows the landing as the limit.

**"With the same gaps and the same end", 2.2 + 3.1: this is the term that failed.** From T on, number 1 takes 154.4 - 26.1 - 115.6 = 12.7 us beyond its work, not 5.3. (1.5 of the difference is mine: the old kernel, counted from its first `UP` as I did with the new one, has 147.5 - 26.1 - 114.6 = 6.8, and I had counted it from `UP,17`.) The sums of the windows from 30 to 130 us, old kernel and number 1, show most of it as gaps of PE:

```profile
sum 100.00, PE 99.86 PEld 81.05 DVE 81.50 ACT 57.31 POOL 50.82; mean PE 9.99 PEld 8.10 DVE 8.15 ACT 5.73 POOL 5.08
```

```profile
sum 100.00, PE 95.49 PEld 76.95 DVE 82.56 ACT 54.15 POOL 59.62; mean PE 9.55 PEld 7.70 DVE 8.26 ACT 5.42 POOL 5.96
```

PE is idle for 4.5 us there instead of 0.1. The old list has PE without a gap; I gave that to a list in which each engine's steps stand in another order. So 165.4 became 172.9 by -2.1 (T), +7.4 (gaps and end) and +2.2 (loads).

**DMA turns and single loads "at nothing, up to 2 us at each".** In the old list the upper end is the right one: four turns with their single loads cost 7.5 us of lag, 1.9 each, through SP's queue. In the new list those of the tiles aren't what costs: taking them back gave nothing (10). For r that isn't shown (11). What makes the 5.9 us over the old kernel's 6.8 is **open**: `PAIRS`, the single loads and `XT` on ACT weren't run by themselves. Number 12 shows one place that, mended, handed its loss to the next.

**What would show it.** The 17 loads and ACT's 16 us are there; `UP,1` is at 28.0, not near 30.8. Of the six waits four are on a relu, but of 1.50 (59.25), 2.72, 2.45 and 1.41 us (104.74, of a `DN`), so two of them are below the 2 to 4 that I named; that of `RS,0` ends with `OT`, and that of `RS,1` is `UP,16`'s. Behind `TL` the lag grows by only 1.2 us to the end. The DMA turn that ended the wait at 82.25 is the kind of row that I had named as speaking against me; it is one of 1.7 us.

No version run here was faster than the old kernel.
